# One SBUF ring with loads of 64 KB rows, and a head's softmax limits worked out between quarters of the next values, in a decode block

## The chip, the cores and the metric

The kernel runs on one core of one Trainium2 chip. The time is device microseconds (us) of that core; a median is over all the runs of a kernel. "Span" is the time of one execution as the hardware profiler shows it; the run's time is 1.7 to 2.3 us longer. PSUM is the memory that PE writes its results to. PE is the matrix engine, DVE the vector engine, ACT the scalar engine, SP the engine that issues the loads here. The core's 16 DMA engines move the data.

## The reference, cut to what matters

One token goes through attention with a long cache and then through a gated feed-forward block:

```python
q = layernorm(x) @ wq                      # 32 heads of 128, wq is 1024 x 4096
scores = q @ k_cache.T * 128**-0.5         # 4 K/V heads, 65536 positions each, bf16
o = softmax(scores) @ v_cache              # 8 query heads share one K/V head
h = x + o @ wo
h2 = h + (gelu(ln(h) @ w_gate) * (ln(h) @ w_up)) @ w_down     # 1024 -> 3584 -> 1024
```

K and V are 67 MB each (64 MiB), the weights some 39 MB: 173 MB are read once and used once.

## The kernel before

Every load goes to one of five buffers of 32 KB per partition. K and V come in units of 128 partitions x 32 KB (4 MB): 16 units of K, 16 of V, four to a head. A K unit is transposed in place on DVE in four quarters, PE makes its scores into one PSUM tile `qk_ps` (a single buffer), ACT copies the scores out, and then DVE takes their maximum. Only then can the next unit's scores begin. A V unit is only multiplied.

```python
chpool = ctx.enter_context(tc.tile_pool(name="chpool", bufs=NBUF))     # NBUF = 5, CW = 16384 bf16 = 32 KB
def load(src, name):
    t = chpool.tile([P, CW], BF16, name=name, tag="ch")
    ...
    nc.sync.dma_start(out=tv, in_=src)

def k_scores(g, li):
    qk_ps = ps_qk.tile([P, 2, 512], F32, name="qk_ps", tag="qkps")     # ps_qk has bufs=1
    for a in range(TG):                                                # 32 matmuls of 512 columns
        ...
def k_keep(g, li):
    ac(nc.scalar.copy(out=sc[:], in_=flat))
    dv(nc.vector.tensor_reduce(out=state[("mx", g)][:, li:li + 1], in_=flat, axis=AX.X, op=ALU.max))

for g in range(1, Hkv):                    # K of head g beside V of head g - 1
    for li in range(NL):
        k_load(g, li)                      # load and four transposes
        v_load(g - 1, li)
        ...
        if li == 0 and g > 1: v_evac(g - 2)        # end of an older head: copies ...
        k_scores(g, li)
        k_keep(g, li)
        if li == 0 and g > 1: v_end(g - 2)         # ... and small float32 matmuls
        if li == NL - 1: softmax_head(g)           # maximum over partitions, bias, exponentials
        v_values(g - 1, li)
```

Of the kernel before, what the change touches and what calls it, by code (L numbers as in the profile page):

```python
# [11 lines left out]
BF16 = mybir.dt.bfloat16  # L12
# [5 lines left out]
def kernel(  # L18
# [13 lines left out]
    nc = tc.nc  # L32
    P = 128
    D = A_x.shape[-1]
# [38 lines left out]
    used = sum(-(-b // 32) * 32 for b in (4 * P, 4 * P, 2 * (W0 + NS * P), 128, 4 * rep, 4 * DC, D // 2, 2 * P,  # L73
                                          64 * DC, 2 * DC, 4, 2 * Hq))
    lead.tile([P, (-(used + 128)) % 4096], mybir.dt.uint8, name="lead_pad")
    chpool = ctx.enter_context(tc.tile_pool(name="chpool", bufs=NBUF))
    const = ctx.enter_context(tc.tile_pool(name="const", bufs=1))
    small = ctx.enter_context(tc.tile_pool(name="small", bufs=2))
    o_fin = const.tile([P, D // 4], BF16, name="o_fin")
# [74 lines left out]
    def tr(out, in_, identity):  # L154
        pe(nc.tensor.transpose(out=out, in_=in_, identity=identity))  # L155

    def load(src, name):
        t = chpool.tile([P, CW], BF16, name=name, tag="ch")
        n, w = src.shape[1], src.shape[2]
        tv = t[:, 0:n * w].rearrange("p (n w) -> p n w", w=w)  # L160
        nc.sync.dma_start(out=tv, in_=src)
        return tv

    wq_v = A_wq.rearrange("(p c) n -> p c n", c=DC)
    WB = max(1, CW // HD)
    assert HD <= CW and DC % WB == 0
    nc.vector.memset(x_row[:], 0.0)
    nc.scalar.dma_start(out=x_row[0:97:32, :], in_=A_x[0, 0].rearrange("(g n) -> g n", g=4))
    wq_tiles = []
    for c0 in range(0, DC, WB):  # L170
        wv = load(wq_v[:, c0:c0 + WB, :], "wq_sb")
        wq_tiles.extend(wv[:, i, :] for i in range(WB))

    make_identity(nc, ident_bf[:])
    make_identity(nc, ident_f[:])
# [84 lines left out]
    v_v = [A_v_cache[0, g].rearrange("(p n) d -> p n d", p=P) for g in range(Hkv)]  # L260

    state = {}
    kv_big = {}

    def kv_load(src_v, li, name):
        return load(src_v[:, li * LN:(li + 1) * LN, :], name)

    NSP = 4
    CP = LN // NSP

    def k_load(g, li):
        kt = kv_load(k_v[g], li, "k_sb").rearrange("p n d -> p (n d)").bitcast(U32)
        w = CP * Dh // 2
        for c in range(NSP):
            dv(nc.vector.transpose(out=kt[:, c * w:(c + 1) * w], in_=kt[:, c * w:(c + 1) * w]))  # L275
        state[("kt", g, li)] = kt.bitcast(BF16).rearrange("p (a k n b i t) -> p a k n b i t", a=TG, k=2, n=16, b=2, i=32)

    def k_scores(g, li):
        kt = state.pop(("kt", g, li))
        qk_ps = ps_qk.tile([P, 2, 512], F32, name="qk_ps", tag="qkps")  # L280
        for a in range(TG):
            for bp in range(4):
                o = W0 + (g * 4 + bp) * P - a * rep
                for k in range(2):
                    mm(qk_ps[:, k, :], wsel[:, o:o + P], kt[:, a, k, :, bp // 2, :, bp % 2],
                       a == 0 and bp == 0, a == TG - 1 and bp == 3, loaded=(k == 1))
        state[("qk", g, li)] = qk_ps
# [8 lines left out]
        dv(nc.vector.tensor_reduce(out=state[("mx", g)][:, li:li + 1], in_=flat, axis=AX.X, op=ALU.max))  # L296
        state[("sc", g, li)] = sc

    def softmax_head(g):
        mx1 = small.tile([P, 1], F32, name="mx1", tag="mx1")  # L300
        dv(nc.vector.tensor_reduce(out=mx1[:], in_=state.pop(("mx", g))[:], axis=AX.X, op=ALU.max))  # L301
        mxT_ps = ps_m.tile([1, P], F32, name="mxT_ps", tag="misc")
        tr(mxT_ps[:], mx1[:], ident_f[:])
        gm = small.tile([1, rep], F32, name="gm", tag="gm")
        dv(nc.vector.tensor_reduce(out=gm[:], in_=mxT_ps[:].rearrange("o (x h) -> o h x", h=rep), axis=AX.X, op=ALU.max))
        gmb = small.tile([1, P // rep, rep], F32, name="gmb", tag="gmb")
        dv(nc.vector.tensor_scalar(out=gmb[:], in0=gm[:].unsqueeze(1).to_broadcast([1, P // rep, rep]),
                                   scalar1=-scale, scalar2=None, op0=ALU.mult))
        nb_ps = ps_m.tile([P, 1], F32, name="nb_ps", tag="misc")
        mm(nb_ps[:], gmb[:].rearrange("o x h -> o (x h)"), ones_f[0:1, 0:1], True, True)  # L310
        nbias = small.tile([P, 1], F32, name="nbias", tag="nbias")
        dv(nc.vector.tensor_copy(out=nbias[:], in_=nb_ps[:]))  # L312
        lpart = small.tile([P, NL], F32, name="lpart", tag="lpart")
        pTs = []
        for li in range(NL):
            pe_r = qkpool.tile([P, 2 * 512], BF16, name="pe_r", tag="qk")
            ac(nc.scalar.activation(out=pe_r[:], in_=state.pop(("sc", g, li))[:], func=ACT.Exp,  # L317
                                    bias=nbias[:, 0:1], scale=scale, accum_out=lpart[:, li:li + 1]))
            pT = ptpool.tile([P, GPL, TG * rep], BF16, name="pT", tag=f"pT{li}")
            dv(nc.vector.transpose(out=pT[:].rearrange("p m c -> p (m c)"), in_=pe_r[:]))  # L320
            pTs.append(pT)
        state[("v", g)] = {"pT": pTs, "lpart": lpart}

    def v_load(g, li):
        state[("v_sb", g, li)] = kv_load(v_v[g], li, "v_sb")

    def v_values(g, li):
        st = state[("v", g)]
        v_sb = state.pop(("v_sb", g, li)).rearrange("p (t m) d -> p m t d", t=TG)
        if li == 0:  # L330
            st["acc"] = ps_acc.tile([P, 4, TG * Dh], F32, name="acc_ps", tag="acc")
        acc, pT = st["acc"], st["pT"][li]
        for m0 in range(0, GPL, 4):
            stat = pT[:, m0:m0 + 4, :].rearrange("p m c -> p (m c)")
            for c in range(4):
                mm(acc[:, c, :].rearrange("p (t d) -> p t d", t=TG), stat, v_sb[:, m0 + c, :, :],
                   li == 0 and m0 == 0, li == NL - 1 and m0 + 4 == GPL, loaded=(c > 0))

    def v_evac(g):
        st = state[("v", g)]  # L340
        acc = st["acc"]
        acc_sb = qkpool.tile([P, TG * Dh], F32, name="acc_sb", tag="qk")
        for c in range(4):
            sl = slice(32 * c, 32 * c + 32)
            if c < 2:
                dv(nc.vector.tensor_copy(out=acc_sb[sl, :], in_=acc[sl, c, :]))  # L346
            else:
                ac(nc.scalar.copy(out=acc_sb[sl, :], in_=acc[sl, c, :]))  # L348
        lsum = small.tile([P, 1], F32, name="lsum", tag="lsum")
        dv(nc.vector.tensor_reduce(out=lsum[:], in_=st["lpart"][:], axis=AX.X, op=ALU.add))  # L350
        lrow = small.tile([P, rep], F32, name="lrow", tag="lrow")
        dv(nc.vector.tensor_scalar(out=lrow[:], in0=hmask[:], scalar1=lsum[:, 0:1], scalar2=None, op0=ALU.mult))
        st["end"] = acc_sb, lrow

    def v_end(g):
        acc_sb, lrow = state[("v", g)]["end"]
        l_ps = ps_m.tile([P, rep], F32, name="l_ps", tag="misc")
        mm(l_ps[:], ones_f[:], lrow[:], True, True)
        rl = small.tile([P, rep], F32, name="rl", tag="rl")
# [3 lines left out]
            mm(o_ps[:], acc_sb[:, t * Dh:(t + 1) * Dh], sel[:, t * rep:(t + 1) * rep], t == 0, t == TG - 1)  # L363
        dv(nc.vector.tensor_tensor(out=oT_all[:, g * rep:(g + 1) * rep], in0=o_ps[:], in1=rl[:], op=ALU.mult))

    for li in range(NL):
        k_load(0, li)
        if li > 0:
            k_keep(0, li - 1)
        k_scores(0, li)  # L370
    for g in range(1, Hkv):
        for li in range(NL):
            k_load(g, li)
            v_load(g - 1, li)
            if li == 0 and g == 1:
                k_keep(0, NL - 1)
                softmax_head(0)
            if li == 0 and g > 1:
                v_evac(g - 2)
            k_scores(g, li)  # L380
            k_keep(g, li)
            if li == 0 and g > 1:
                v_end(g - 2)
            if li == NL - 1:
                softmax_head(g)
            v_values(g - 1, li)
    v_evac(Hkv - 2)
    v_end(Hkv - 2)
    for li in range(NL):
        v_load(Hkv - 1, li)  # L390
        v_values(Hkv - 1, li)
    v_evac(Hkv - 1)
    v_end(Hkv - 1)

# [34 lines left out]
    assert Hq % WN == 0  # L429
    at_ps = [row_bank("at_ps") for _ in range(DS)]  # L430
    for wc in range(Hq // WN):
        wv = load(wo_v[:, wc * WN:(wc + 1) * WN, :], "wo_sb")
        for cc in range(WN):
            c = wc * WN + cc
            row_mm(at_ps, o2z[:, c, :], wv[:, cc, :], c, c < 4, c + 4 >= Hq)
# [45 lines left out]
    def up_mm(banks, w, c, loaded):  # L481
        for s in range(NF):
# [2 lines left out]
               w.rearrange("p (m j) -> p m j", j=FC)[:, :, 4 * s:4 * s + 4],  # L485
               c == 0, c == DC - 1, loaded=(loaded or s >= 4), tile_position=(0, 32 * g))

    for c0 in range(0, DC, GB):
        wg = load(gv[:, c0:c0 + GB, :], "wg_sb")
        wu = load(uv[:, c0:c0 + GB, :], "wu_sb")  # L490
        last = c0 + GB == DC
        for cc in range(GB):
            up_mm(g_banks, wg[:, cc, :], c0 + cc, False)
            if not last:
                up_mm(u_banks, wu[:, cc, :], c0 + cc, True)
    g_t = turned(g_banks, "wg")
    for cc in range(GB):
        up_mm(u_banks, wu[:, cc, :], c0 + cc, False)
    g_ap = rows.tile([P, FC], F32, name="g_ap")
    for j0, nj, src in g_t:  # L500
        nc.vector.tensor_copy(out=by_j(g_ap, j0, nj), in_=src)
# [16 lines left out]
    actz = padded(rows, act_bf[:], FC, "actz")  # L518
    c0 = 0
    for sz in sizes:  # L520
        wv = load(wd_v[:, c0:c0 + sz, :], "wd_sb")
        for cc in range(sz):
            c = c0 + cc
            out_mm(actz[:, c, :], lambda g: wv[:, cc, g * OW:(g + 1) * OW], False, c + 1 == FC)
        c0 += sz
# [32 lines left out]
```

## Time and profile before

| | before |
|---|---|
| runs, us | 408.62 to 408.82, median 408.82 |
| span, us | 407.0 |
| last data landed (packet records of the trace), us | 403.14 |
| load queue | 6488 packets, 173.02 MB, 98.8% of 16 engines |

These are lines of the page of the kernel before. The rows of digits are tenths of busy time in 40 equal slices of the span, PEclk is the clock granted to PE in tenths, GB/s what the DMA engines moved; the q1 line has packets, MB and the share of 16 engines' span; the last line is the chain of waits by engine.

```profile
span 407.0 us, 2658 instructions
PE 299.3 (74%) x1481; PEld 62.8 (15%) x713; DVE 202.6 (50%) x185; ACT 44.9 (11%) x67; POOL 7.4 (2%) x17
PEclk9965778969999989899989898999868899866565
DMA  9999999999999999999999999999999999999995
GB/s 364 461 412 451 423 419 457 410 454 422 414 461 415 441 430 415 461 415 444 427 419 457 415 448 425 420 454 415 448 426 432 440 419 444 424 429 442 426 421 220
q1 hardware_dynamic: 6488, 173.02, 98.8%
DMA 46%; PE 30%; DVE 18%; ACT 4%; issue 2%; SPq 0%; ACTq 0%; DVEq 0%
```

The DMA row has no slice below 9 tenths but the last. No engine comes near that. The chain of waits does pass through PE and DVE, but there it only tells when a buffer became free. The DMA issues of the page (number, size, us from issue to landing):

```profile
k_sb<-in_A_k_cache_dram SPq DMA_DIRECT2D x16, 4096.0 KB, 33.6
v_sb<-in_A_v_cache_dram SPq DMA_DIRECT2D x16, 4096.0 KB, 37.1
```

A load of 4 MB takes 9.7 us of the DMA engines, so at 34 to 37 us two to three others are queued ahead of it. In this document the **lead** of a load is the time from its issue to its first packet, from the trace's packet records. The first load of the program, which finds an empty queue, has a lead of 1.02 us. Before the change no later load of K or V had a lead under 13 us.

### The profile page before, as it was taken

The numbers are of one execution on the slowest core, as the hardware profiler recorded it, in microseconds if no ns is written. First come the engines' busy times: TensorE is split into PE (matmuls) and PEld (weight loads), VectorE is DVE, ScalarE is ACT, GpSimd is POOL, SyncE is SP. The second block draws the span as 40 slices with busy tenths as digits, with TensorE's granted clock in tenths as the row PEclk, the third lists the DMA queues.
The fourth block names the chain that finished last, engine by engine and source line by source line (L and its number), as shares of the span: only waits on it lengthen the run. The fifth ranks groups of instructions, "written<-read, shape, count | busy, mean of one in ns | idle before, by whom it ended". The sixth has DMA issues, their size and how long they took to land.

```text
span 407.0 us, 2658 instructions
## 1 busy us (share of the span) xinstructions
PE 299.3 (74%) x1481; PEld 62.8 (15%) x713; DVE 202.6 (50%) x185; ACT 44.9 (11%) x67; POOL 7.4 (2%) x17
## 2 busy tenths in 40 slices
PE   0356298769997788897956969978767998725564
PEld 0011011111110111111101121110112110200233
DVE  1118989876673678555464968181843001110110
ACT  1010000150000041000002320000051000100000
POOL 2000000000000000000000000000010000100000
PEclk9965778969999989899989898999868899866565
DMA  9999999999999999999999999999999999999995
GB/s 364 461 412 451 423 419 457 410 454 422 414 461 415 441 430 415 461 415 444 427 419 457 415 448 425 420 454 415 448 426 432 440 419 444 424 429 442 426 421 220
DMA packets 6508, 173.19 MB, mean 426 GB/s; under 512 B 728, under 2 KB 736, under 8 KB 992
## 3 DMA queue, kind: packets, MB, share of 16 engines
q1 hardware_dynamic: 6488, 173.02, 98.8%
q8 instruction: 8, 0.13, 0.1%
q14 instruction: 4, 0.03, 0.0%
q10 hardware_dynamic: 8, 0.00, 0.0%
HBM read 173.02 MB, written 0.00 MB: 425 GB/s over the span
## 4 chain that ended last, share of the span: by engine, by line
DMA 46%; PE 30%; DVE 18%; ACT 4%; issue 2%; SPq 0%; ACTq 0%; DVEq 0%
DMA k_sb<-in_A_k_cache_dram 32%; DVE k_sb L275 12%; PE acc_ps L146 12%; DMA wg_sb<-in_B_w_gate_dram 8%; PE qk_ps L144 6%; PE qk_ps L146 6%; DMA wd_sb<-in_B_w_down_dram 5%; PE acc_ps L144 4%; DVE mx L296 2%; ACT sc L295 2%; DVE pT L320 1%; ACT pe_r L317 1%; PE o_ps L144 1%; DVE acc_sb L346 1%; ACT acc_sb L348 1%
## 5 line engine op out<-in xcount | busy, mean ns | idle before, releaser
L275 DVE STREAM_TRANSPOSE k_sb<-k_sb 128x2048 uint32<-128x2048 uint32 x64 | 142.1, 2278 | 34.5 <-DMA k_sb<-in_A_k_cache_dram 34.5
L144 PE MATMUL qk_ps<-k_sb,wsel 128*128 128x512 bf16 x256 | 103.9, 406 | 36.3 <-DVE k_sb L275 23.8
L146 PE MATMUL acc_ps<-v_sb,pT 128*128 128x512 bf16 x384 | 112.6, 405 | 0.0
L146 PE MATMUL qk_ps<-k_sb,wsel 128*128 128x512 bf16 x256 | 103.7, 405 | 0.0
L144 PE MATMUL acc_ps<-v_sb,pT 128*128 128x512 bf16 x128 | 52.0, 406 | 0.0
L144 PEld LDWEIGHTS <-wsel 128*128 128x128 bf16 x256 | 26.0, 102 | 141.3 <-issue 121.2
L296 DVE TENSOR_REDUCE mx<-qk_ps 128x1 f32<-128x1024 f32 x16 | 19.5, 1219 | 43.9 <-ACT sc L295 43.9
L295 ACT COPY sc<-qk_ps 128x1024 f32<-128x1024 f32 x16 | 16.2, 1012 | 201.7 <-PE qk_ps L146 201.6
L144 PEld LDWEIGHTS <-pT 128*128 128x128 bf16 x128 | 13.6, 106 | 99.8 <-issue 99.7
L320 DVE STREAM_TRANSPOSE pT<-pe_r 128x1024 bf16<-128x1024 bf16 x16 | 19.0, 1226 | 6.2 <-ACT pe_r L317 6.2
L346 DVE COPY acc_sb<-acc_ps 32x512 f32<-32x512 f32 x8 | 5.4, 672 | 32.7 <-PE acc_ps L146 32.7
L317 ACT ACTIVATE pe_r<-sc,nbias 128x1024 bf16<-128x1024 f32 x16 | 18.2, 1140 | 14.3 <-DVE nbias L312 13.6
L146 PE MATMUL wu_ps<-wu_sb,hnz 128*32 128x512 bf16 x40 | 7.1, 572 | 7.5 <-DMA wu_sb<-in_B_w_up_dram 7.5
L348 ACT COPY acc_sb<-acc_ps 32x512 f32<-32x512 f32 x8 | 4.6, 577 | 62.0 <-DVE acc_sb L346 61.9
L232 DVE COPY wg_ev<-wg_ps 128x512 f32<-128x512 f32 x1 | 0.7, 690 | 20.9 <-PE wg_ps L144 20.9
L144 PE MATMUL q_ps<-wq_sb,xnz 128*32 128x512 bf16 x32 | 5.2, 626 | 8.0 <-DMA wq_sb<-in_A_wq_dram 8.0
L144 PE MATMUL f_ps<-wd_sb,actz 128*32 128x256 bf16 x112 | 6.9, 413 | 5.3 <-DMA wd_sb<-in_B_w_down_dram 5.3
L144 PE MATMUL wg_ps<-wg_sb,hnz 128*32 128x512 bf16 x32 | 6.5, 598 | 5.3 <-DMA wg_sb<-in_B_w_gate_dram 5.3
L144 PE MATMUL o_ps<-sel,acc_sb 128*128 128x8 f32 x32 | 5.2, 290 | 6.7 <-DVE rl L360 5.9
L144 PE MATMUL ln_tot<-ln_s,ones_f 128*128 128x1 f32 x8 | 1.9, 311 | 10.8 <-DVE ln_s L194 9.0
L155 PE MATMUL mxT_ps<-ident_f,mx 128*1 128x128 f32 x4 | 1.3, 322 | 11.1 <-DVE mx L301 11.1
L232 DVE COPY q_ev<-q_ps 128x512 f32<-128x512 f32 x1 | 0.7, 691 | 13.5 <-PE q_ps L146 13.5
(102 smaller groups left out, 87.6 us busy)
## 6 DMA issues: line engine op xcount, KB each, us to landing
k_sb<-in_A_k_cache_dram SPq DMA_DIRECT2D x16, 4096.0 KB, 33.6
v_sb<-in_A_v_cache_dram SPq DMA_DIRECT2D x16, 4096.0 KB, 37.1
wq_sb<-in_A_wq_dram SPq DMA_DIRECT2D x2, 4096.0 KB, 16.5
wo_sb<-in_A_wo_dram SPq DMA_DIRECT2D x2, 4096.0 KB, 30.8
wg_sb<-in_B_w_gate_dram SPq DMA_DIRECT2D x2, 3584.0 KB, 32.0
wu_sb<-in_B_w_up_dram SPq DMA_DIRECT2D x2, 3584.0 KB, 33.1
wd_sb<-in_B_w_down_dram SPq DMA_DIRECT2D x1, 3584.0 KB
wd_sb<-in_B_w_down_dram SPq DMA_DIRECT2D x1, 1792.0 KB, 24.8
```

The lines of the kernel that those rows point to most:

```text
L144: return pe(t.matmul(out, lhsT=lhsT, rhs=rhs, start=start, stop=stop, tile_position=tile_position, skip_group_check=skip_group_check))
L146: op = t.add_instruction(mybir.InstMatmult(name=nc.get_next_instruction_name(), engine=t.engine, start_tensor_calc=start, stop_tensor_calc ...
L155: pe(nc.tensor.transpose(out=out, in_=in_, identity=identity))
L232: nc.vector.tensor_copy(out=dst, in_=src)
L275: dv(nc.vector.transpose(out=kt[:, c * w:(c + 1) * w], in_=kt[:, c * w:(c + 1) * w]))
L295: ac(nc.scalar.copy(out=sc[:], in_=flat))
L296: dv(nc.vector.tensor_reduce(out=state[("mx", g)][:, li:li + 1], in_=flat, axis=AX.X, op=ALU.max))
L317: ac(nc.scalar.activation(out=pe_r[:], in_=state.pop(("sc", g, li))[:], func=ACT.Exp, bias=nbias[:, 0:1], scale=scale, accum_out=lpart[:, ...
L320: dv(nc.vector.transpose(out=pT[:].rearrange("p m c -> p (m c)"), in_=pe_r[:]))
L346: dv(nc.vector.tensor_copy(out=acc_sb[sl, :], in_=acc[sl, c, :]))
L348: ac(nc.scalar.copy(out=acc_sb[sl, :], in_=acc[sl, c, :]))
```

## The change

Its intent is fewer packets. The five buffers become one tile of five units, so a load can cover two neighbouring units with rows of 64 KB. Some of the K and V loads become so long, and `wq` too; `w_gate` becomes one load with rows of 56 KB. The order of K and V is redone so that the pairs fit. The first quarter of a following K unit is transposed ahead of the maximum of the present one. The maximum over partitions and the bias of a head are worked out between quarters of the next values. The core of the diff:

```diff
-    chpool = ctx.enter_context(tc.tile_pool(name="chpool", bufs=NBUF))
+    chpool = ctx.enter_context(tc.tile_pool(name="chpool", bufs=1))
+    ring = chpool.tile([P, NBUF * CW], BF16, name="ring")
...
+    todo = [("k", 0, 0, 1), ("k", 0, 1, 1), ("k", 0, 2, 1), ("k", 0, 3, 1), ("k", 1, 0, 1),
+            ("v", 0, 0, 2), ("k", 1, 1, 1), ("k", 1, 2, 2), ("v", 0, 2, 2),
+            ("k", 2, 0, 1), ("v", 1, 0, 2), ("k", 2, 1, 2), ("v", 1, 2, 1), ("k", 2, 3, 1), ("v", 1, 3, 1),
+            ("k", 3, 0, 2), ("v", 2, 0, 1), ("k", 3, 2, 2), ("v", 2, 1, 2), ("v", 2, 3, 1),
+            ("v", 3, 0, 2), ("v", 3, 2, 2)]            # what, head, first unit, units in the load
...
+        turn_up_to(u, 4)
+        if g > 1 and li == 0:
+            v_evac(g - 2)
+        if units[n + 1][0] == "k":
+            turn_up_to(units[n + 1], 1)
+        k_scores(g, li)
...
+        k_keep(g, li)
+        if g > 1 and li == 0:
+            v_end(g - 2)
...
     def v_values(g, li, between=()):
...
+            if m0 == 4 and between:
+                between[0](g + 1)      # maximum, transpose to one row
+            if m0 == 12 and between:
+                between[1](g + 1)      # bias, exponentials
```

More of the change, by code (lines that the diff above doesn't have):

```diff
@@ L155, in tr, with load @@
         pe(nc.tensor.transpose(out=out, in_=in_, identity=identity))
-    def load(src, name):
-        t = chpool.tile([P, CW], BF16, name=name, tag="ch")
+    at = [0]
+    def load(src, off=0):
         n, w = src.shape[1], src.shape[2]
-        tv = t[:, 0:n * w].rearrange("p (n w) -> p n w", w=w)
-        nc.sync.dma_start(out=tv, in_=src)
-        return tv
+        units = -(-(off + n * w) // CW)
+        o = at[0] * CW + off
+        assert o + n * w <= NBUF * CW
+        at[0] = (at[0] + units) % NBUF
+        tv = ring[:, o:o + n * w]
+        nc.sync.dma_start(out=tv.rearrange("p (n w) -> p n w", w=w), in_=src)
+        return tv.rearrange("p (n w) -> p n w", w=w)
     wq_v = A_wq.rearrange("(p c) n -> p c n", c=DC)
-    WB = max(1, CW // HD)
-    assert HD <= CW and DC % WB == 0
     nc.vector.memset(x_row[:], 0.0)
     nc.scalar.dma_start(out=x_row[0:97:32, :], in_=A_x[0, 0].rearrange("(g n) -> g n", g=4))
-    wq_tiles = []
-    for c0 in range(0, DC, WB):
-        wv = load(wq_v[:, c0:c0 + WB, :], "wq_sb")
-        wq_tiles.extend(wv[:, i, :] for i in range(WB))
+    assert DC * HD == 2 * CW
+    wq_t = load(wq_v[:])
+    wq_tiles = [wq_t[:, c, :] for c in range(DC)]
     make_identity(nc, ident_bf[:])
@@ L262, with kv_load, k_turn @@
     state = {}
-    kv_big = {}
-    def kv_load(src_v, li, name):
-        return load(src_v[:, li * LN:(li + 1) * LN, :], name)
+    def kv_load(what, g, li, n):
+        t = load((k_v if what == "k" else v_v)[g][:, li * LN:(li + n) * LN, :])
+        for u in range(n):
+            state[(what, g, li + u)] = t[:, u * LN:(u + 1) * LN, :]
     NSP = 4
     CP = LN // NSP
-    def k_load(g, li):
-        kt = kv_load(k_v[g], li, "k_sb").rearrange("p n d -> p (n d)").bitcast(U32)
+    def k_turn(g, li, parts=range(4)):
+        kt = state[("k", g, li)].rearrange("p n d -> p (n d)").bitcast(U32)
         w = CP * Dh // 2
-        for c in range(NSP):
+        for c in parts:
             dv(nc.vector.transpose(out=kt[:, c * w:(c + 1) * w], in_=kt[:, c * w:(c + 1) * w]))
-        state[("kt", g, li)] = kt.bitcast(BF16).rearrange("p (a k n b i t) -> p a k n b i t", a=TG, k=2, n=16, b=2, i=32)
     def k_scores(g, li):
-        kt = state.pop(("kt", g, li))
+        kt = state.pop(("k", g, li)).rearrange("p n d -> p (n d)").rearrange(
+            "p (a k n b i t) -> p a k n b i t", a=TG, k=2, n=16, b=2, i=32)
         qk_ps = ps_qk.tile([P, 2, 512], F32, name="qk_ps", tag="qkps")
@@ L297, in k_keep, with softmax_turn @@
         state[("sc", g, li)] = sc
-    def softmax_head(g):
+    def softmax_turn(g):
         mx1 = small.tile([P, 1], F32, name="mx1", tag="mx1")
@@ L303, in softmax_head, with softmax_rest @@
         tr(mxT_ps[:], mx1[:], ident_f[:])
+        state[("mxT", g)] = mxT_ps
+    def softmax_rest(g):
+        mxT_ps = state.pop(("mxT", g))
         gm = small.tile([1, rep], F32, name="gm", tag="gm")
@@ L321, in softmax_head, with v_values @@
             pTs.append(pT)
-        state[("v", g)] = {"pT": pTs, "lpart": lpart}
-    def v_load(g, li):
-        state[("v_sb", g, li)] = kv_load(v_v[g], li, "v_sb")
-    def v_values(g, li):
-        st = state[("v", g)]
-        v_sb = state.pop(("v_sb", g, li)).rearrange("p (t m) d -> p m t d", t=TG)
+        state[("vs", g)] = {"pT": pTs, "lpart": lpart}
+    def v_values(g, li, between=()):
+        st = state[("vs", g)]
+        v_sb = state.pop(("v", g, li)).rearrange("p (t m) d -> p m t d", t=TG)
         if li == 0:
@@ L337, in v_values @@
                    li == 0 and m0 == 0, li == NL - 1 and m0 + 4 == GPL, loaded=(c > 0))
+            if m0 == 4 and between:
+                between[0](g + 1)
+            if m0 == 12 and between:
+                between[1](g + 1)
     def v_evac(g):
-        st = state[("v", g)]
+        st = state[("vs", g)]
         acc = st["acc"]
@@ L355, in v_end @@
     def v_end(g):
-        acc_sb, lrow = state[("v", g)]["end"]
+        acc_sb, lrow = state[("vs", g)]["end"]
         l_ps = ps_m.tile([P, rep], F32, name="l_ps", tag="misc")
@@ L364, in v_end, with turn_up_to @@
         dv(nc.vector.tensor_tensor(out=oT_all[:, g * rep:(g + 1) * rep], in0=o_ps[:], in1=rl[:], op=ALU.mult))
-    for li in range(NL):
-        k_load(0, li)
-        if li > 0:
-            k_keep(0, li - 1)
-        k_scores(0, li)
-    for g in range(1, Hkv):
-        for li in range(NL):
-            k_load(g, li)
-            v_load(g - 1, li)
-            if li == 0 and g == 1:
-                k_keep(0, NL - 1)
-                softmax_head(0)
-            if li == 0 and g > 1:
-                v_evac(g - 2)
-            k_scores(g, li)
-            k_keep(g, li)
-            if li == 0 and g > 1:
-                v_end(g - 2)
-            if li == NL - 1:
-                softmax_head(g)
-            v_values(g - 1, li)
-    v_evac(Hkv - 2)
-    v_end(Hkv - 2)
-    for li in range(NL):
-        v_load(Hkv - 1, li)
-        v_values(Hkv - 1, li)
+    assert NL == 4 and NBUF == 5
+    todo = [("k", 0, 0, 1), ("k", 0, 1, 1), ("k", 0, 2, 1), ("k", 0, 3, 1), ("k", 1, 0, 1),
[4 rows of a table added]
+    units = [(what, g, li) for what, g, l0, n in todo for li in range(l0, l0 + n)]
+    size = {(what, g, l0): n for what, g, l0, n in todo}
+    turned_parts = {}
+    def turn_up_to(u, m):
+        have = turned_parts.get(u, 0)
+        if u in size and not have:
+            kv_load(*u, size[u])
+        k_turn(u[1], u[2], range(have, m))
+        turned_parts[u] = m
+    for n, (what, g, li) in enumerate(units):
+        u = (what, g, li)
+        if what == "v":
+            if u in size:
+                kv_load(*u, size[u])
+            if g == Hkv - 1 and li == 0:
+                v_evac(g - 1)
+                v_end(g - 1)
+            due = ("mx", g + 1) in state and ("sc", g + 1, NL - 1) in state
+            v_values(g, li, (softmax_turn, softmax_rest) if due else ())
+            continue
+        turn_up_to(u, 4)
[4 more added lines that the diff above has]
+        k_scores(g, li)
+        if g == 1 and li == 0:
+            softmax_turn(0)
+            softmax_rest(0)
+        k_keep(g, li)
+        if g > 1 and li == 0:
+            v_end(g - 2)
     v_evac(Hkv - 1)
@@ L431 @@
     for wc in range(Hq // WN):
-        wv = load(wo_v[:, wc * WN:(wc + 1) * WN, :], "wo_sb")
+        wv = load(wo_v[:, wc * WN:(wc + 1) * WN, :])
         for cc in range(WN):
@@ L486, in up_mm @@
                c == 0, c == DC - 1, loaded=(loaded or s >= 4), tile_position=(0, 32 * g))
+    wg = load(gv[:])
+    for c in range(DC):
+        up_mm(g_banks, wg[:, c, :], c, False)
+    g_t = turned(g_banks, "wg")
     for c0 in range(0, DC, GB):
-        wg = load(gv[:, c0:c0 + GB, :], "wg_sb")
-        wu = load(uv[:, c0:c0 + GB, :], "wu_sb")
-        last = c0 + GB == DC
+        wu = load(uv[:, c0:c0 + GB, :])
         for cc in range(GB):
-            up_mm(g_banks, wg[:, cc, :], c0 + cc, False)
-            if not last:
-                up_mm(u_banks, wu[:, cc, :], c0 + cc, True)
-    g_t = turned(g_banks, "wg")
-    for cc in range(GB):
-        up_mm(u_banks, wu[:, cc, :], c0 + cc, False)
+            up_mm(u_banks, wu[:, cc, :], c0 + cc, False)
     g_ap = rows.tile([P, FC], F32, name="g_ap")
@@ L520 @@
     for sz in sizes:
-        wv = load(wd_v[:, c0:c0 + sz, :], "wd_sb")
+        at[0] = 0
+        wv = load(wd_v[:, c0:c0 + sz, :], c0 * D)
         for cc in range(sz):
```

## The prediction

> **What bounds it now.** The DMA queue. The page's row of DMA shares reads 9 tenths in all but the last of 40 slices; its queue lines give the load queue 98.8% of 16 engines' span for 173.02 MB. By the trace's packets all 16 engines are busy from 1.0 to about 400 us, with under 1 us of holes; the last data lands at 403.1 of 407.0 us. Behind it stand only 12 small matmuls (1.04 us), a copy (0.42 us) and the store (chain of waits). PE (74%), DVE (50%) and ACT (11%) have room. The k_sb transposes and score matmuls in the chain only say when a buffer is freed: a load is issued 34 to 37 us before it lands (DMA issues) and one of 4 MB takes about 9.7 us, so two to three are always queued. By the issue times the queue never comes closer than an estimated 13.6 us to running dry.
>
> **What the change can save.** The bytes stay. In the trace's packets a 32 KB row takes 1213 ns, 28 KB 1062, 14 KB 535, 8 KB 309, 4 KB 159: a straight line of 27.2 bytes/ns per engine (435 GB/s for 16) plus about 8 ns a packet; a semaphore packet takes 9 ns. The Trainium skill, "DMA: Bandwidth & Descriptors", section "Where 436 GB/s comes from", puts the ports' ceiling at 435.2 GB/s; this slope sits on it, so only the 8 ns can go. An engine serves 8 rows of a load. Twelve loads of 64 KB rows save each engine 12 x (8 x 8 + 9) = 0.9 us, the gate load (56 KB rows) 0.07 us: an estimate of 1.0 us, all on the critical path, if a 64 KB row is one packet. If it is cut in two, 0.1 us.
>
> **What it adds and moves.** A double load waits for two units, so it is issued later. With measured durations (transposes of a unit 8.9 us, maximum 1.2, scores or values of a unit 6.9 warm, up to 11 cold) I worked the new order through: the closest calls are double loads into units that hold two K units, issued an estimated 7 to 9 us before need. So no hole. The whole wq load starts the q matmuls at 21.7 us (half began at 12.1); q is spread by about 32 us, and the first K lands at 31.4: nothing lost. Moving maximum and bias into the next values takes a stall of about 2 us per head off PE, which doesn't bound: 0. The tail keeps its five wd loads: about 4 us after the last data, as before.
>
> **Prediction.** 408.8 - 1.0 = 407.8 us, range 406.8 to 409.0. Faster by over 2%: 0.01; within 2%: 0.96; slower by over 2%: 0.03.
>
> **What would show it right.** About 4,600 packets instead of 6,488 on the load queue, 64 KB packets of about 2418 ns, share still near 98 to 99%, mean rate up by about 1 GB/s; PE's waits for mxT and nb gone; the DMA row at 9 everywhere.
>
> **What would make it wrong.** 64 KB rows cut into two packets (then 408.7) or served more slowly. A hole because a double load is issued too late, most likely at 95 to 150 us, where a half-clocked PE could stretch the scores: each hole adds its full length. One ring tile could make loads wait for more than the units they overwrite; the built wait lists show no sign of it.

## The result and the profile after

| | before | after |
|---|---|---|
| runs, us | 408.61 to 408.82, median 408.72 | 408.64 to 411.31, median 409.74 |
| ratio | 1 | 1.0026, 95% interval 1.0004 to 1.0047 |
| span of the profiled run, us | 407.0 | 407.0 |
| packets on the load queue | 6488 | 4760 |
| last data landed in that run, us | 403.14 | 403.02 |

A ratio is the mean time of one kernel's runs over that of the other's of the same rounds, so not quite the ratio of the medians. The predicted microsecond was not gained, one was lost, and the runs, which agreed within 0.2 us, now differ by 2.7 us.

The same lines of the page after. The profiled run happened to be one of the quickest (408.97 us):

```profile
span 407.0 us, 2631 instructions
PE 293.6 (72%) x1481; PEld 61.9 (15%) x729; DVE 202.4 (50%) x185; ACT 44.8 (11%) x67; POOL 7.4 (2%) x17
PEclk9996899998986899888999968998998989985966
DMA  9999999999999999999999999999999999999995
GB/s 412 412 412 454 420 419 460 413 451 459 419 425 419 444 451 420 432 425 432 415 451 443 435 448 419 438 427 419 458 419 444 427 415 432 448 436 409 440 413 206
q1 hardware_dynamic: 4760, 173.02, 98.6%
DMA 52%; PE 30%; DVE 14%; ACT 3%; issue 1%; ACTq 0%
```

Packets fell as intended, and a packet of 64 KB has a median of 2418 ns, as predicted. Yet the span is the same to 0.04 us. This page shows no hole and no cause. The issues show a first sign; these are the K and V loads that still have rows of 32 KB (the page lists the others only in part):

```profile
ring<-in_A_k_cache_dram SPq DMA_DIRECT2D x8, 4096.0 KB, 36.0
ring<-in_A_v_cache_dram SPq DMA_DIRECT2D x4, 4096.0 KB, 29.2
```

They are as early as before. The long loads are not. Leads in the packet records of this run, in us: V 0-1 of head 0 14.0, K 2-3 of head 1 10.4, V 2-3 of head 0 10.4, **V 0-1 of head 1 2.4**, K 1-2 of head 2 6.6, K 0-1 of head 3 4.9, K 2-3 of head 3 11.6, **V 1-2 of head 2 2.6**, V 0-1 of head 3 4.8, V 2-3 of head 3 8.4.

### The profile page after: what moved, and what is told of

It is laid out like the page before. It is cut to its first block, busy times and chain, and to the rows that moved or that the text cites. A ratio compares the mean times of both kernels' runs of the same rounds, so it can differ in the third digit from the quotient of the medians.

```text
span 407.0 us, 2631 instructions
## 1 busy us (share of the span) xinstructions
PE 293.6 (72%) x1481; PEld 61.9 (15%) x729; DVE 202.4 (50%) x185; ACT 44.8 (11%) x67; POOL 7.4 (2%) x17
## 3 DMA queue, kind: packets, MB, share of 16 engines
q1 hardware_dynamic: 4760, 173.02, 98.6%
## 4 chain that ended last, share of the span: by engine, by line
DMA 52%; PE 30%; DVE 14%; ACT 3%; issue 1%; ACTq 0%
DMA ring<-in_A_k_cache_dram 30%; DVE ring L279 10%; PE qk_ps L145 9%; PE qk_ps L147 9%; PE acc_ps L147 8%; DMA ring<-in_A_v_cache_dram 7%; DMA ring<-in_B_w_down_dram 7%; DMA ring<-in_B_w_gate_dram 7%; DVE mx L300 3%; PE acc_ps L145 3%; ACT sc L299 3%; PE wg_ps L145 0%; PE wg_ps L147 0%; PE f_ps L145 0%; PE nb_ps L145 0%
## 5 line engine op out<-in xcount | busy, mean ns | idle before, releaser
L279 DVE STREAM_TRANSPOSE ring<-ring 128x2048 uint32<-128x2048 uint32 x64 | 142.4, 2280 | 36.3 <-DMA ring<-in_A_k_cache_dram 36.3
L145 PE MATMUL qk_ps<-ring,wsel 128*128 128x512 bf16 x256 | 105.9, 414 | 42.6 <-DVE mx L300 25.6
L147 PE MATMUL acc_ps<-ring,pT 128*128 128x512 bf16 x384 | 109.2, 395 | 0.0
L147 PE MATMUL qk_ps<-ring,wsel 128*128 128x512 bf16 x256 | 105.6, 413 | 0.0
L145 PE MATMUL acc_ps<-ring,pT 128*128 128x512 bf16 x128 | 51.0, 398 | 7.0 <-DMA ring<-in_A_v_cache_dram 4.1
L145 PEld LDWEIGHTS <-wsel 128*128 128x128 bf16 x256 | 26.5, 103 | 148.6 <-issue 131.7
L145 PE MATMUL q_ps<-ring,xnz 128*32 128x512 bf16 x32 | 4.5, 537 | 9.4 <-DMA ring<-in_A_wq_dram 9.4
L145 PE MATMUL f_ps<-ring,actz 128*32 128x256 bf16 x112 | 5.6, 351 | 6.2 <-DMA ring<-in_B_w_down_dram 6.2
L145 PE MATMUL wu_ps<-ring,hnz 128*32 128x512 bf16 x32 | 4.6, 502 | 7.0 <-DMA ring<-in_B_w_up_dram 7.0
L145 PE MATMUL wg_ps<-ring,hnz 128*32 128x512 bf16 x32 | 5.2, 582 | 5.9 <-DMA ring<-in_B_w_gate_dram 5.9
L145 PEld LDWEIGHTS <-hnz 128*32 128x32 bf16 x64 | 3.3, 120 | 19.6 <-issue 17.0
```

The source lines that it names most:

```text
L145: return pe(t.matmul(out, lhsT=lhsT, rhs=rhs, start=start, stop=stop, tile_position=tile_position, skip_group_check=skip_group_check))
L147: op = t.add_instruction(mybir.InstMatmult(name=nc.get_next_instruction_name(), engine=t.engine, start_tensor_calc=start, stop_tensor_calc ...
L279: dv(nc.vector.transpose(out=kt[:, c * w:(c + 1) * w], in_=kt[:, c * w:(c + 1) * w]))
```

## The experiments

Three theories. **A, late issue**: a double load waits for two units, and the chain that frees them is so long that small changes of pace leave DMA without work. **B, long rows**: 64 KB rows are themselves served less evenly. **C, unequal engines**: the 16 DMA engines finish at different times for reasons of their own. "Quick" stands below for runs of up to about 409.1 us, "late" for those over 409.3 us. All kernels gave correct results, but for e_half.

| run | what it is | runs, us | median | ratio to before, 95% interval |
|---|---|---|---|---|
| after_again | the change again | 408.92 to 411.30 | 409.78 | 1.0028 (1.0013 to 1.0042) |
| e_single | K and V in 32 KB rows, new order | 408.75 to 409.11 | 408.91 | 1.0002 (0.9990 to 1.0014) |
| e_split5 | the five loads with short leads split | 408.40 to 408.78 | 408.59 | 0.9994 (0.9982 to 1.0007) |
| e_half | half of the transposes, wrong result | 408.41 to 411.05 | 409.99 | 1.0023 (1.0005 to 1.0041) |
| e_tight | only those five long | 408.54 to 410.55 | 408.68 | 1.0005 (0.9992 to 1.0019) |
| e_warm | filling matmuls | 409.82 to 411.59 | 410.50 | 1.0041 (1.0029 to 1.0054) |
| e_more | 1.2 us more DVE work a K unit | 414.17 to 414.61 | 414.31 | 1.0136 (1.0121 to 1.0151) |
| after_look | the change, one look | 411.26 (one run, state unknown) | | |
| e_one | one load split | 408.71 to 409.08 | 408.86 | 1.0000 (0.9986 to 1.0015) |
| e_vend | all loads long, one block of work moved | 408.47 to 409.10 | 408.97 | 0.9999 (0.9985 to 1.0014) |
| e_soft | before, with the softmax move alone | 408.63 to 408.94 | 408.70 | 0.9997 (0.9985 to 1.0010) |
| e_more1 | e_single with e_more's work | 408.79 to 408.92 | 408.85 | 1.0000 (0.9984 to 1.0017) |

The kernel before had medians of 408.75 to 408.84 us beside them.

**after_again.** No edit.

> The changed kernel again, to see its spread on another chip and a second trace. Theory A (late issue): the loads of 64 KB rows into two units that held two K units, or a K and a V unit, were issued only 2.4 to 6.6 us before their first packet (v head 1 at 144.3 us, v head 2 at 260.3 us, K head 3 at 209.7 us, v head 3 at 287.2 us), so small changes in compute time, above all of the granted clock, open holes: runs spread over 1 us or more, median 409 to 410, and a trace of a slow run has part-idle stretches in the DMA row near 145, 216, 263 or 291 us. Theory B (rows): 64 KB rows themselves are served less evenly: the spread is there without any hole, slow packets are scattered over all loads of 64 KB rows.

The spread is there again (chip 10). Its trace was again that of the quickest run, with leads of 3.8 and 2.8 us at the two loads; it decides nothing between the theories.

**e_single.** All K and V loads are split, in the same order of work:

```diff
+    todo = [(what, g, l0 + i, 1) for what, g, l0, n in todo for i in range(n)]
     units = [(what, g, li) for what, g, l0, n in todo for li in range(l0, l0 + n)]
```

> The changed kernel with every K and V load of 64 KB rows split into two of 32 KB rows, same units, same order of work; wq and the gate stay whole. Theory A: issue comes earlier than need by over 10 us everywhere, runs agree within 0.3 us, time 408.6 to 408.9 (no packet saved but wq's and the gate's). Theory B: the same, since the rows are gone; but if the order of work (softmax between quarters, first quarter ahead of the maximum) were the cause, it stays at 409.5 or more with the spread.

As expected of A and B. The new order, the early first quarter and the softmax move together cost nothing and give nothing.

**e_split5.** The five loads with leads under 7 us are split, the other five long ones, wq and the gate stay:

```diff
+    tight = [("v", 1, 0), ("k", 2, 1), ("k", 3, 0), ("v", 2, 1), ("v", 3, 0)]
+    todo = [(what, g, l0 + i * n // m, n // m) for what, g, l0, n in todo
+            for m in [n if (what, g, l0) in tight else 1] for i in range(m)]
```

> Only the five loads of 64 KB rows that were issued less than 7 us before their first packet are split into two (v head 1 first pair, K head 2 second and third, K head 3 first pair, v head 2 second and third, v head 3 first pair); six K and V loads, wq and the gate keep long rows. Theory A: tight runs, 408.2 to 408.6, a little under the kernel before. Theory B: the excess shrinks only in proportion, 409.2 or so with a spread of 1 us.

The spread falls from 2.4 to 0.4 us with half of the long K and V loads kept. That fits A. The median is 0.2 us below the kernel before, but the interval holds 1.

**e_half.**

```diff
         for c in parts:
+            if c % 2:
+                continue
             dv(nc.vector.transpose(out=kt[:, c * w:(c + 1) * w], in_=kt[:, c * w:(c + 1) * w]))
```

> WRONG RESULT ON PURPOSE: two of the four transposes of each K unit are left out, all loads stay as in the changed kernel. VectorE work per K unit falls from 8.9 to about 4.5 us, so units are freed earlier. Theory A: margins at the tight loads grow to about 8 us or more, runs agree within 0.3 us, time 407.9 to 408.3, the saving that I predicted less the part that overlaps. Theory B: no change, 409 to 410 with a spread of over 1 us, for the rows are the same.

Time and spread did not move, as B had it. But this run did not turn the knob that it was built to turn: V 0-1 of head 1 was issued at 144.03 us instead of 144.29. Its DVE timeline shows why (start, us busy, group, and in brackets the idle time before and what ended it):

```profile
123.51 4.48 DVE L281 STREAM_TRANSPOSE ring<-ring 128x2048 uint32<-128x2048 uint32 x2
134.13 1.22 DVE L302 TENSOR_REDUCE mx<-qk_ps 128x1 f32<-128x1024 f32 x1 [6.14 <-ACT sc L301]
```

DVE now waits 6 us for PE's scores. The chain that frees a pair of K units runs through PE, ACT and the single PSUM tile, not through the transposes. So by its times e_half tells nothing between A and B. It tells where the prediction's pacing was wrong. Its trace tells more: it fell in a late run (410.54 us), and V 1-2 of head 2 was issued at 262.35 us with a lead of 0.99 us, that of an empty queue.

**e_tight.** The complement of e_split5:

```diff
+    todo = [(what, g, l0 + i, 1 if (what, g, l0) not in tight else n) for what, g, l0, n in todo
+            for i in range(1 if (what, g, l0) in tight else n)]
```

> The complement of e_split5: only the five loads of 64 KB rows that are issued late (under 7 us before their first packet) stay whole, the other six of K and V are split into two of 32 KB rows; wq and the gate stay whole. Theory A (late issue): nearly all of the loss and the spread come back, median 409.3 to 410, range over 1 us. Theory B (long rows as such): the loss shrinks with the number of long rows, about half of that of the changed kernel, 409.2 or less.

A's number was missed: four of six runs were at 408.5 to 408.7, two at 409.35 and 410.55. The late runs came back, but fewer. In its trace only one of the five loads still had a lead under 4 us: V 1-2 of head 2, 2.7 us. That narrowed A to this one load.

**after_look.** No edit; it fell in a late run.

> The changed kernel once more for one more trace: if it falls in a slow execution (over 409.5), theory A wants holes at the late loads in it, theory B slow packets of 64 KB anywhere, and a third theory (C) unequal finishing of the 16 DMA engines at the end.

This is the trace that was missing: the changed kernel itself in a late run. First the SP and ACT timelines around V 1-2 of head 2, in the quick run of the changed kernel. The two ACT copies from qk_ps end the scores of K 0 and K 1 of head 3; the acc_sb copies before them belong to the end of head 1:

```profile
246.44 1.17 ACT L357 COPY acc_sb<-acc_ps 32x512 f32<-32x512 f32 x2 [12.78 <-DVE acc_sb L355]
247.63 1.01 ACT L299 COPY sc<-qk_ps 128x1024 f32<-128x1024 f32 x1
260.34 1.01 ACT L299 COPY sc<-qk_ps 128x1024 f32<-128x1024 f32 x1 [11.69 <-PE qk_ps L147]
...
260.33 7.24 SPq L167 DMA_DIRECT2D ring<-in_A_v_cache_dram  x2
```

The same in the late run:

```profile
246.33 1.17 ACT L357 COPY acc_sb<-acc_ps 32x512 f32<-32x512 f32 x2 [12.85 <-DVE acc_sb L355]
248.38 1.01 ACT L299 COPY sc<-qk_ps 128x1024 f32<-128x1024 f32 x1 [0.88 <-PE qk_ps L147]
262.25 1.01 ACT L299 COPY sc<-qk_ps 128x1024 f32<-128x1024 f32 x1 [12.86 <-PE qk_ps L147]
...
262.25 7.24 SPq L167 DMA_DIRECT2D ring<-in_A_v_cache_dram  x2
```

In both runs K 0-1 of head 3, whose two units this load overwrites, had landed at 235.7 us. The SP line follows the end of the second score block at once: 260.33 in the quick run, 262.25 in the late one. The next packet is due at about 263 us in both. The lead is 2.6 us in one and 0.96 us in the other, which is that of an empty queue. What DMA did from 262 to 268 us (the view of stretches; the last three numbers are PE's granted clock, DMA's share and GB/s), quick run first:

```profile
262.00:268.00 6.00, 5.69 (x28) 0.68 (x7) 3.47 (x3) 0.00 (x0) 0.00 (x0) 1.00 1.05 448
```

and the late run:

```profile
262.00:268.00 6.00, 6.00 (x29) 0.69 (x7) 4.05 (x3) 1.01 (x1) 0.00 (x0) 1.00 1.01 374
```

The share still reads 1.01, because most of the loss lies inside packets that began and were slow: only the rate gives it away. (Packets are counted where they start, so one stretch is rough.) By the packet records the late span is 2.28 us longer than the quick one. Averaged over 16 engines, 1.18 us of this are packets longer than the median of their size, mostly the first ones after 263 us and a run of smaller delays until 310 us; 0.28 us are engines without a packet at 263; 0.73 us more is spent at the end, where engines that are done wait for the slowest. That sums to 2.19. The Trainium skill, "DMA: Bandwidth & Descriptors", section "Why a DMA increments its semaphore by 16 and not by 1", says that the engines of a DMA finish independently; the trace agrees, the last landing comes 0.72 us after the engines' mean before the change, 0.94 in the quick run and 1.67 in the late run. Why an empty queue should leave the engines more unequal at the end was not tested.

Why the second block ended 1.9 us later is seen on PE. (0.75 us of it was there before: the first block's copy began at 248.38 instead of 247.63 us.) In the quick run:

```profile
250.52 1.03 PE L145 MATMUL o_ps<-sel,acc_sb 128*128 128x8 f32 x8 [3.29 <-DVE rl L369]
254.92 0.49 PE L147 MATMUL qk_ps<-ring,wsel 128*128 128x512 bf16 x1
255.25 0.38 PE L145 MATMUL qk_ps<-ring,wsel 128*128 128x512 bf16 x1
255.47 0.38 PE L147 MATMUL qk_ps<-ring,wsel 128*128 128x512 bf16 x1
```

In the late run:

```profile
250.91 1.75 PE L145 MATMUL o_ps<-sel,acc_sb 128*128 128x8 f32 x8 [2.45 <-DVE rl L369]
252.51 0.59 PE L145 MATMUL qk_ps<-ring,wsel 128*128 128x512 bf16 x1
252.90 0.63 PE L147 MATMUL qk_ps<-ring,wsel 128*128 128x512 bf16 x1
257.59 0.51 PE L145 MATMUL qk_ps<-ring,wsel 128*128 128x512 bf16 x1
257.94 0.38 PE L147 MATMUL qk_ps<-ring,wsel 128*128 128x512 bf16 x1
```

A score matmul takes 0.63 us at the slow rate (started every 0.43 us) and 0.38 us at the full one (every 0.22 us). After the idle gap PE is slow until 254.9 us in the quick run and until 257.6 us in the late one, and there the eight small o_ps matmuls are slow too, 1.75 instead of 1.03 us. The Trainium skill, "TensorE: Matmul & The Clock Gate", section "Part 1: The HAM clock gate", says that PE falls to half rate after an idle window of about 3.4 us and that this window is "free-running", so the point of change shifts from run to run. The traces agree. They record the granted clock: in every kept trace each change of it falls, within 0.01 us, on a grid of steps of 3.41 us, and the grid lies elsewhere in each run. Two views of stretches cut along it (the third number from the end is the granted clock), quick run first:

```profile
251.73:255.15 3.42, 3.42 (x10) 0.58 (x4) 3.42 (x3) 0.00 (x0) 0.00 (x0) 0.50 1.02 441
255.15:258.56 3.41, 3.41 (x16) 0.67 (x7) 3.21 (x2) 0.00 (x0) 0.00 (x0) 1.00 1.11 480
```

and the late run:

```profile
251.02:254.43 3.41, 3.41 (x13) 1.86 (x11) 1.73 (x2) 0.00 (x0) 0.00 (x0) 0.50 0.97 423
254.43:257.84 3.41, 3.41 (x9) 0.58 (x4) 3.41 (x3) 0.00 (x0) 0.00 (x0) 0.50 0.89 384
```

One window at half rate in the quick run, two in the late one. The other traces with this load whole and the end of head 1 in its place fit: after the end of the first block the late e_half and e_warm have two windows at half rate (251.1 to 258.0 and 250.2 to 257.0 us), the quick e_tight has one (251.7 to 255.1) and the quick after_again none. No run set the position of the grid, so that it alone makes a run quick or late is inferred.

**e_warm.** Filling matmuls before seven score blocks were to keep PE at full rate:

```diff
+    FILL = {(1, 2): 40, (1, 3): 10, (2, 1): 10, (2, 2): 10, (3, 0): 28, (3, 1): 4, (3, 3): 10}
...
+        if FILL.get((g, li)):
+            d_ps = ps_d.tile([P, 512], F32, name="d_ps", tag="d")
+            for i in range(FILL[(g, li)]):
+                mm(d_ps[:], wsel[:, W0:W0 + P], wsel[:, 0:512], True, True, loaded=(i > 0))
```

> All loads of the changed kernel stay. 112 idle-filling matmuls of 128x512 into a spare PSUM bank stand before seven score blocks, so that PE does not fall to half its clock while it waits (in the changed kernel the scores of K 2 and 3 of head 1 took 9.9 and 8.6 us, at full clock 6.9). Results unchanged. Theory A: v head 1 is issued about 3 to 5 us earlier than at 144.3, v head 2 earlier than at 260.3, the spread falls to 0.4 us or so, median 408.2 to 408.7. Theory B: no change, 409.5 to 410 with the same spread.

The result is the opposite of what I expected of A: 410.5 us. The idea failed, but the time still follows the issue. V 0-1 of head 1 came only 1.3 us earlier (142.95), and V 1-2 of head 2 came later, at 262.54 us with a lead of 0.95: the four fillers before K 1 of head 3 themselves ran at the slow rate, from 252.2 to 253.6 us, right in the chain, and the scores behind them were slow all the same.

**e_more.** A sixteenth of each K unit is transposed twice more, which leaves the result as it is:

```diff
-            dv(nc.vector.transpose(out=kt[:, c * w:(c + 1) * w], in_=kt[:, c * w:(c + 1) * w]))
+            for again in range(3 if c == 0 else 1):
+                z = slice(c * w, c * w + w // 4) if again < 2 and c == 0 else slice(c * w, (c + 1) * w)
+                dv(nc.vector.transpose(out=kt[:, z], in_=kt[:, z]))
```

> The changed kernel with about 1.2 us more of VectorE work on each K unit: a sixteenth of the unit is transposed and transposed back before its first quarter is transposed. Results unchanged. Theory A: the two loads with 2.4 and 2.6 us before their first packet come about 1.2 us later, so DMA gets holes near 147 and 263 us: median 410.5 or more. Theory B: no change, 409.7.

The time rose to 414.3 us, and the hole is now large enough for the page:

```profile
span 412.2 us, 2661 instructions
DMA  9999999999999999999999999898999999999994
GB/s 407 407 423 442 424 439 449 458 397 429 479 420 420 404 467 428 420 426 420 429 450 432 410 467 432 320 407 369 446 446 464 409 407 432 446 441 406 428 417 185
```

The row of DMA shares has two 8s, and the rates of 320, 407 and 369 GB/s are those of 258 to 289 us. V 1-2 of head 2 was issued at 266.38 us, after DMA had begun to run out. By the packet records the engines were idle for 3.42 us there; longer packets (1.18 us) and the end (0.51) make up nearly all the rest of the 5.2 us over the quick run of the changed kernel.

**e_more1.** The control: the same extra work with the loads of e_single.

> Control for e_more (414.3 us): the same extra 1.2 us of VectorE work on each K unit, but with every K and V load split into rows of 32 KB as in e_single. If the work itself costs time, it is about as slow as e_more. Theory A: the units come free one by one, no load is late, 408.7 to 409.2.

408.85 us. The extra work by itself costs nothing; behind double loads it costs 4.5 us (414.31 against the 409.78 of after_again). B has no place for that, since the rows of e_more are those of the changed kernel.

**e_one.** Only V 1-2 of head 2 is split:

```diff
+    todo = [(what, g, l0 + i, n // m) for what, g, l0, n in todo
+            for m in [2 if (what, g, l0) == ("v", 2, 1) else 1] for i in range(m)]
```

> The changed kernel with one load split: values 2 and 3 of head 2, which in the slow trace was issued at 262.25 us, 0.96 us before its first packet (fast traces 260.2 to 260.3, 2.6 to 2.8 us before), and left holes there. The other eleven loads of 64 KB rows stay. Theory A, narrowed to this one load: the slow executions vanish, median 408.2 to 408.6, range under 0.5 us. Theory B (long rows as such): only a twelfth of the loss goes, 409.6 with the spread. Theory C (unequal finishing of the DMA engines for its own reasons): no change.

The range of its four runs falls to 0.4 us with ten of eleven long loads kept. The loss of 1 us is gone, but the median, 408.86, is not the gain that I had still expected.

**e_vend.** All long loads stay. The end of head 1 is moved from behind the first to behind the second K unit of head 3:

```diff
-        if g > 1 and li == 0:
+        if g > 1 and li == g - 2:
             v_evac(g - 2)
...
-        if g > 1 and li == 0:
+        if g > 1 and li == g - 2:
             v_end(g - 2)
```

> All twelve loads of 64 KB rows stay. Only the end of head 1 (copies of the accumulator, two sums, eight small float32 matmuls) is moved from behind the first to behind the second K unit of head 3; there it stood between the two score blocks whose end releases the late load. Theory A: the load of values 2 and 3 of head 2 is issued about 1.5 to 2.5 us earlier (258 to 260 us), slow executions vanish, median 408.1 to 408.5, range under 0.6 us. Theories B and C: 409.5 to 410 with the spread, as the rows are untouched.

Its ACT and SP lines at the same place:

```profile
247.76 1.01 ACT L299 COPY sc<-qk_ps 128x1024 f32<-128x1024 f32 x1 [14.17 <-PE qk_ps L147]
257.98 1.17 ACT L357 COPY acc_sb<-acc_ps 32x512 f32<-32x512 f32 x2 [9.21 <-DVE acc_sb L355]
259.17 1.01 ACT L299 COPY sc<-qk_ps 128x1024 f32<-128x1024 f32 x1
...
258.61 13.09 SPq L167 DMA_DIRECT2D ring<-in_A_v_cache_dram  x2
```

The acc_sb copies now stand at the end of the second score block (its last matmul ends at 258.6 us), the small matmuls behind it, and the load is issued at 258.61 us with a lead of 4.1 us. The late runs are gone: 408.47 to 409.10 in four runs, and e_one's four were under 409.1 too, while 10 of the changed kernel's 13 runs were over 409.4. No row was touched, so the lost microsecond was the late issue of one load, not the rows. The four runs still gain nothing over the kernel before, and the next load, V 0-1 of head 3, has a lead of only 2.5 us now.

**e_soft.** The kernel before, with `softmax_head` cut in two and called between quarters of the last V unit of a head, as in the diff above.

> The kernel BEFORE with one part of the change alone: maximum and bias of heads 1 to 3 worked out between quarters of the next values. I predicted it worth 0: 408.6 to 408.9, ratio 1.000 within 0.001; in the trace PE's waits at mxT and nb are gone.

408.70 us: worth 0, as predicted. PE's waits for the maximum, before (us in total, times, longest):

```profile
PE mxT_ps L155 <- DVE mx L301: 11.1, 4, 3.0
PE nb_ps L144 <- DVE gmb L307: 2.9, 4, 0.7
```

and with the move alone:

```profile
PE mxT_ps L155 <- DVE mx L301: 5.5, 4, 2.6
PE nb_ps L144 <- DVE gmb L311: 0.7, 1, 0.7
```

The waits are halved or better, not gone (that part of the expectation was too strong): 7.8 us less of waiting on PE, and no time gained, for PE is not what bounds.

## Why the prediction was wrong, point by point

- **Right:** DMA bounds; a 64 KB row is one packet of 2418 ns; the packets fall (to 4760; I had said 4,600, for one long load too many); the softmax move is worth 0; if a hole came, it would be from a double load into two K units, issued too late with PE at half rate. That last point stood in the prediction as its risk, and I gave it too little weight; I had looked for it at 95 to 150 us, and it came at 263.
- **The step that failed: "issued an estimated 7 to 9 us before need. So no hole."** Measured leads were 2.4 to 3.8 us at two loads in quick runs and 0.96 us at one of them in a late run. In my working, I had let a pair of K units go at the pace of DVE. The chain is serial through one PSUM tile. In the quick run for K 0-1 of head 3: landed 235.7, first quarter transposed 238.5, scores 238.6 to 247.1, copy, maximum and the end of head 1 to 251.4, scores 251.4 to 260.3, issue 260.3. That is 24.6 us from landing to issue, 26.5 in the late run. DMA needed the load after 27 us, and about 1 us passes from issue to first packet. The cost of a hole was wrong too: I had said that it adds its full length, but in the late run 0.28 us without packets came with 2.28 us of time. e_vend and e_one took the late runs away and e_more made them the rule.
- **The mis-sized term: the saving of 1.0 us.** From load to load, an engine takes 9.68 us for 8 rows of 32 KB and 19.32 us for 8 rows of 64 KB, so a double load saves 19.36 - 19.32 = 0.04 us, not the 0.073 that I had summed from packet lengths. Neighbouring packets overlap a little (8 rows of 1213 ns and the semaphore packet take 9.68 us, 1210 ns a row). I had also counted twelve such loads where there are eleven. Eleven times 0.04 and 0.05 us of the gate make about 0.5 us.
- **Where the 0.5 us stays in quick runs.** In the one that was profiled the last data landed 0.12 us earlier (403.02 us against 403.14). Longer packets (0.16 us more) and more waiting for the slowest engine at the end (0.22 us more) take the rest. Why these two grew was not tested. e_split5, with no lead of K or V under 7.5 us, was 0.2 us below the kernel before by medians, which its interval cannot tell from nothing.
- **The range** of 406.8 to 409.0 left out the very case that I had named. Leads of 7 us on a schedule worked out by hand, with PE at either of two rates, deserved a tail to 412.

No kernel tried beats the one before beyond doubt; e_split5 is the best candidate.

## What to carry to other kernels

When DMA bounds, compute the lead of every load, and take it from the whole serial chain that frees its buffer (score, copy, maximum, next score), with the matrix engine at its slow rate; a load over two buffers waits for the later of them. Before merging loads, ask what a packet costs from start to start, not how long it lasts: here a merge of two 4 MB loads was worth 0.04 us and put up to 2.5 us at risk. If a tuned kernel's runs begin to scatter after a change, get the trace of a slow run: the quick run's page looked the same as before.

## What the Trainium skill lacked or had wrong

- "TensorE: Matmul & The Clock Gate", section "Part 1": it gives an idle window of about 3.4 us before the half rate. In the changed kernel an idle gap of 2.4 us (133.07 to 135.49 us) was followed by half rate, while in e_vend a gap of 2.36 us before 250.08 us was followed by full rate. A gap shorter than the window can be enough: the window on the clock's grid that held the first gap (132.27 to 135.68 us) had PE busy for 0.99 of 3.41 us and was followed by half rate, the one that held most of the second (246.21 to 249.62 us) had it busy for 1.51 us and was not.
- "DMA: Bandwidth & Descriptors": its measured sizes are those of whole transfers; it gives no time of a row of 32 or 64 KB. Here rows of 32 KB take 1210 ns from start to start on average over a load, rows of 64 KB 2415 ns, so rows beyond 32 KB gain about 0.2%.
- No page says what happens when a queue runs empty in the middle of a stream: after the gap at 263 us in the late run most of the first 64 KB packets were 0.4 to 1.1 us longer than the median of 2418 ns, much like the first packets of the program (0.3 to 0.9 us longer in the quick run).
